# Attention and two expert layers in one kernel: the second pair's queries and keys ahead of the first weights, and the first chunk's tokens split block by block

## The chip, the cores and the metric

The kernel runs on one core of one Trainium2 chip. Times are device microseconds (us) of one execution, as the median of the runs shown; the trace of one further execution shows where its time goes. A core has five engines that run programs of their own and meet at semaphores: TensorE (PE, with PEld for the loading of its stationary operand), VectorE (DVE), ScalarE (ACT), GpSimd (POOL) and SyncE (SP). SP computes nothing here; it issues the transfers between the device's memory and the core's memory.

## The reference

```python
# q, k, v: (4, 8, 576, 64)  f32;  M_prev: (4, 8, 64, 64);  z_prev: (4, 8, 64);  beta: (8)
scores = q @ k.T / sqrt(64), causal;   a = softmax(scores);   local = a @ v
phi(x) = where(x > 0, x, exp(x) - 1) + 1
mem_out = (phi(q) @ M_prev) / (phi(q) @ z_prev + 1e-6)
g = sigmoid(beta);  attn = g * mem_out + (1 - g) * local          # per head
x = attn as (2304 tokens, 512)
x = (sigmoid(x @ w_gate) * (x @ w_val)) @ w_out                   # 512 -> 1536 -> 512
h = x @ w_in;  out = (h * clip(h + 3, 0, 6) / 6) @ moe2_w_out     # 512 -> 2048 -> 512
```

## The kernel before

Work on PE is written out by hand (a manual schedule for PE alone); the instructions of DVE, ACT, POOL and SP are put in order by the scheduler that builds the program, so an edit can move them far from where it stands in the code. Once built, each engine goes through its own list in order.

**Phase A** computes attention and, between its pieces, the first layer for the first chunks of tokens. Attention goes by *visits*: a visit is one pair of heads of one batch and one of two ranges of query rows (range 0: rows 0 to 319; range 1: rows 320 to 575). The first four visits are the four pairs of batch 0 in range 0, the next four the same pairs in range 1, then batch 1, and so on. A visit takes two *steps* of the loop in `phase_a`; `t` counts them, from 0. A step issues on PE the scores of one or two blocks of rows (`score_part`, L344, tiles `s`), the transposes of the weights of step t-3 (`transpose_bank`, L402, tiles `t`), the product with the values of step t-4 (`pv`, L426), and *fill*: units of the first layer (`moe`). A unit is three matmuls (`mm3`, L233 to L235), because a float32 operand is split into a high and a low part, and five units stand in a step while the first chunk is worked on (`FILL`). DVE takes the maximum of each row of scores out of PSUM (`row_max`, L324), ACT the exponentials (L362).

`load_visit(v)` issues the loads of a visit: the transposed queries and keys (`qk`, L257 and L258), for a batch's first visit the memory's norms (`zz`), the queries in natural layout (the first part of `aux`, L272, read by `prep_phi`, L297) and the values (L274). `w_load` issues the loads of a group of two blocks of weights into one of two stage buffers (`wst`, L142, 512 KB each); `w_convert` rebuilds the floats out of 64-bit patterns and splits them (L152 to L164). Nine groups are converted in phase A.

The first layer goes by chunks of 312 tokens. Chunk 0 needs batch 0's range 0 of all four pairs, so the last `pv` that it needs is that of visit 3, at t = 11. Each `pv` is copied out (`xpr`, L435), written to device memory (`xd`, L438 to L440) and read back as a block of 128 features (`xc`, L464); ACT and DVE split the block into its two parts (`split`, L228 and L229, tiles `xs0` to `xs3`, one for each pair of heads). `moe_x(c)` does that for all four blocks once `ready(c)` holds, and the first unit of the chunk may stand `LEAD` = 2 steps later. With these rules chunk 0's first unit stands at t = 14 and, after 72 units, its last at t = 28; chunk 1's blocks are asked for at t = 28 and its first unit stands at t = 30.

Phase B finishes the first layer, phase C computes the second.

Of the kernel before, what the change touches and what calls it, by code (L numbers as in the profile page):

```python
# [17 lines left out]
B, H, S, D = 4, 8, 576, 64  # L18
NT, DM = B * S, H * D
FF1, FF2 = 12, 16  # L20
KT = DM // 128
# [31 lines left out]
LAG, LEAD = 1, 2  # L53
# [25 lines left out]
class Kernel:  # L79
# [9 lines left out]
    def setup(self):  # L89
        nc, tc, ctx = self.nc, self.tc, self.ctx  # L90
        cp = self.pool(ctx, "const", 1)
        self.wpool = self.pool(ctx, "wslots", NW_A)
        self.xd = tc.dram_tile([KT, 128, NT], F32, name="xd")
        self.x2p = tc.dram_tile([KT, 128, NT], F32, name="x2p")
        self.x2 = tc.dram_tile([KT, 128, NT], F32, name="x2")
        self.wd = tc.dram_tile([NPAIR, 3, 128, 2048], F32, name="wd")
        self.bt_sb = cp.tile([128, H // 2 * 5], F32, name="bt_sb")
        nc.sync.dma_start(self.bt_sb, self.bt)
        self.three = cp.tile([128, 1], F32, name="three")
        nc.vector.memset(self.three, 3.0)  # L100

    def attn_consts(self, pool):
        nc = self.nc
        self.ident = pool.tile([128, 128], F32, name="ident")
        make_identity(nc, self.ident)
        self.mask = pool.tile([128, 576], F32, name="mask")
        nc.gpsimd.memset(self.mask, 0.0)
        nc.gpsimd.affine_select(
            out=self.mask[:, 448:576],
            in_=self.mask[:, 448:576],  # L110
            compare_op=ALU.is_ge,
            fill=-BIG,
            base=0,
            pattern=[[-1, 128]],
            channel_multiplier=1,
        )
        self.mask0 = pool.tile([128, 64], F32, name="mask0")
        for g in range(2):
            rows = slice(64 * g, 64 * g + 64)
            nc.gpsimd.tensor_copy(self.mask0[rows], self.mask[rows, 448 + 64 * g : 512 + 64 * g])  # L120
        self.a1 = pool.tile([128, H // 2 * 5], F32, name="a1")
        self.a2 = pool.tile([128, H // 2 * 5], F32, name="a2")
        nc.scalar.activation(self.a1, self.bt_sb, AF.Exp)
        nc.scalar.activation(self.a2, self.bt_sb, AF.Exp, scale=-1.0)
        nc.vector.tensor_scalar_add(self.a1, self.a1, 1.0)
        nc.vector.tensor_scalar_add(self.a2, self.a2, 1.0)
# [119 lines left out]
    def load_visit(self, v):  # L246
        if v >= len(VISITS):
            return
        nc = self.nc
        p, ranges = VISITS[v]  # L250
        b, h = PAIRS[p]
        qk = self.pa2.tile([128, 2, S], F32, name="qk", tag="qk")
        a = self.pa2.tile([128, 15 * D], F32, name="aux", tag="aux", bufs=3)
        rg = ranges[0]
        (t0, n), nb, j1 = RTOK[rg], len(ROWS[rg]), RANGES[rg][-1] + 1
        src = self.aux[b, h // 2]
        nc.sync.dma_start(qk[:, 0, t0 : t0 + n], self.qk[b, h // 2, :, 0, t0 : t0 + n])  # L257
        nc.sync.dma_start(qk[:, 1, : t0 + n], self.qk[b, h // 2, :, 1, : t0 + n])  # L258
        if h == 0 and rg == 0:
            z = self.pa2.tile([128, H + H // 2, D], F32, name="zz", tag="zz", bufs=1)  # L260
            flat = lambda t: t.rearrange("p h d -> p (h d)")
            one = lambda t: t.rearrange("o h d -> o (h d)")
            nc.sync.dma_start(flat(z[:, 0:H]), one(self.zz[b : b + 1, 0:H]).broadcast_to([128, H * D]))
            for g in range(2):
                h0 = H + H // 2 * g
                nc.sync.dma_start(
                    flat(z[64 * g : 64 * g + 64, H:]),
                    one(self.zz[b : b + 1, h0 : h0 + H // 2]).broadcast_to([64, H // 2 * D]),
                )
            self.z = z  # L270
        q0 = 0 if rg == 0 else 5 * D
        nc.sync.dma_start(a[:, 0 : nb * D], src[:, q0 : q0 + nb * D])  # L272
        v0 = 5 * D
        nc.sync.dma_start(a[:, v0 : v0 + j1 * 2 * D], src[:, 9 * D : 9 * D + j1 * 2 * D])  # L274
        self.visits[v] = {
            "pair": PAIRS[p],
            "ranges": ranges,
            "z": self.z,
            "qk": qk,
            "qn": a[:, 0 : nb * D].rearrange("p (r d) -> p r d", d=D),  # L280
            "v": a[:, 5 * D :].rearrange("p (j c) -> p j c", j=5),
        }
# [173 lines left out]
        need = (b, 0 if t1 < RTOK[0][1] else 1)  # L456
        return need in self.done and self.step >= self.done[need] + LAG

    def moe_x(self, c):

        xs = []
        for k in range(KT):
            x = self.pm2.tile([128, CA], F32, name="xc", tag="xc")
            self.nc.sync.dma_start(x, self.xd[k, :, c * CA : c * CA + CA])  # L464
            t = self.pm1.tile([128, 2, CA], F32R, name=f"xs{k}", tag=f"xs{k}")
            self.split(t[:, 0], t[:, 1], x, self.nc.scalar, self.nc.vector)
            xs.append((t[:, 0], t[:, 1]))
        self.xnext = (c, xs, self.step)

    def moe_a(self, c):  # L470

# [36 lines left out]
    def phase_a(self):  # L508
        nc, tc = self.nc, self.tc
# [6 lines left out]
        self.plan_weights(keys, [self.wpool] * NW_A)  # L516
        steps = [(v, rg, u[-1]) for v, (p, ranges) in enumerate(VISITS) for rg in ranges for u in UNITS[rg]]
        nt = len(steps)
        self.xnext = None
        stream, c = None, 0  # L520
        tq, vq = [], []

        def moe(k):
            nonlocal stream, c
            while k > 0:
                if stream is None:
                    if c == NCA:
                        return
                    if self.xnext is None or self.xnext[0] != c:
                        if not self.ready(c):  # L530
                            return
                        self.moe_x(c)
                    if self.step < self.xnext[2] + LEAD:
                        return
                    stream = self.moe_a(c)
                    c += 1
                try:
                    next(stream)
                    k -= 1
                except StopIteration:  # L540
                    stream = None

        def transposes(t, k):
            for _ in range(k):
                if tq and tq[0][0] <= t:
                    a = tq.pop(0)[1]
                    self.transpose_bank(*a)
                    if a[2] == len(BANKS[a[1]]) - 1:
                        vq.append((t + 1, a[:2]))

        t = self.step = 0
        sched = tc.manual_schedule(engines={mybir.EngineType.PE})
        sched.__enter__()
        self.load_visit(0)
        self.w_load()
        self.load_visit(1)
        while t < nt or tq or vq:
            self.step = t
            fill = FILL[max(c - 1, 0)]
            first = w = 0  # L560
            if t < nt:
                v, rg, i = steps[t]
                if i == UNITS[rg][0][-1]:
                    self.new_weights(v, rg)
                w = 64 + 128 * i
                first = w if w <= 512 else 320
                self.score_part(v, i, 0, first)
            if t == 0:
                self.prep_phi(0)
            if t < nt and i == RANGES[rg][-1]:  # L570
                self.memory_rows(v, rg)
            transposes(t, 2)
            if vq and vq[0][0] <= t:
                self.pv(*vq.pop(0)[1])
            if first < w or (tq and tq[0][0] <= t):
                moe(fill // 2)
                fill -= fill // 2
                if first < w:
                    self.score_part(v, i, first, w)
                transposes(t, 1)  # L580
            if t < nt:
                self.exponentials(v, i)
                if i == RANGES[rg][-1]:
                    self.normalize(v, rg, 5 <= t < 27)
                    tq += [(t + 3, (v, rg, j)) for j in range(len(BANKS[rg]))]
            moe(fill)
            if t < nt and i == UNITS[rg][0][-1]:
                self.load_visit(v + 2)
            if t < nt and i == RANGES[rg][-1]:
                self.prep_phi(v + 1)  # L590
            if t >= 5 and t % 2:
                self.w_convert()
            if len(self.wstaged) < 2:
                self.w_load()
            t += 1
# [20 lines left out]
        while c < NCA or stream is not None:  # L616
            self.step += 1
            moe(8)
            if n < NW_B - NLATE - 2:
                self.w_next()  # L620
                n += 1
# [352 lines left out]
```

## Time and profile before

| what | value |
|---|---|
| median of 3 runs (lowest to highest) | 1067.75 us (1067.61 to 1069.07) |
| the profiled execution's own time | 1067.68 us |
| its span in the trace | 1065.9 us |
| PE busy | 1029.6 us (97%) |
| DVE, ACT, POOL busy | 645.5 (61%), 550.8 (52%), 83.5 us (8%) |

The span is 1.8 us shorter than the time of the same execution, so a microsecond of the span is a microsecond of the time. Busy shares are means over the whole span; the first 60 us look different from the rest, and PE's few idle microseconds lie mostly there.

### The profile page before, as it was taken

How to read it: one execution, taken by the hardware profiler on the slowest of the kernel's cores; microseconds unless marked ns; L12 is line 12 of the kernel's file. 1: busy time of each engine (PE TensorE's matmuls, PEld its weight loads, DVE VectorE, ACT ScalarE, POOL GpSimd, SP SyncE). 2: the span in 40 equal slices, each digit the busy share in tenths (PEclk: the TensorE clock that was granted, in tenths of full speed). 3: DMA queues.
4: the chain of work that ended last, by engine and by line, in shares of the span. 5: the costliest groups of instructions: out<-in, count | busy, mean ns of one | idle time of the engine just before them, and what ended most of it. 6: DMA issues, size and time to landing. Idle time of an engine off the chain costs nothing.

```text
span 1065.9 us, 16031 instructions
## 1 busy us (share of the span) xinstructions
PE 1029.6 (97%) x5824; PEld 886.0 (83%) x5824; DVE 645.5 (61%) x1543; ACT 550.8 (52%) x1191; POOL 83.5 (8%) x102
## 2 busy tenths in 40 slices
PE   5689999999999999999999999999999999999998
PEld 3367678878887899999888888888888888888886
DVE  6989755454455438888888888743454433643432
ACT  5999875576556644435444343433453333633432
POOL 3212211110111000000000000310002000000000
PEclk9999999999999999999999999999999999999999
DMA  7756542424242215336686877444404542044511
GB/s 227 215 177 198 189 126 75 137 80 123 68 125 79 62 47 179 119 119 250 231 295 246 310 261 275 152 158 188 148 30 158 217 155 103 10 164 172 218 40 60
DMA packets 66239, 164.87 MB, mean 155 GB/s; under 512 B 8432, under 2 KB 41712, under 8 KB 60272
## 3 DMA queue, kind: packets, MB, share of 16 engines
q1 hardware_dynamic: 66160, 163.85, 44.8%
q8 instruction: 46, 0.75, 0.3%
q14 instruction: 33, 0.27, 0.1%
HBM read 122.76 MB, written 41.06 MB: 154 GB/s over the span
## 4 chain that ended last, share of the span: by engine, by line
PE 84%; DVE 5%; ACT 5%; DMA 4%; issue 1%; SPq 1%; POOL 1%; ACTq 0%; POOLq 0%; DVEq 0%
PE acc L822 18%; PE pa L787 9%; PE pb L787 7%; PE m L233 6%; PE m L234 5%; PE m L235 5%; PE g L235 5%; PE g L233 5%; PE g L234 5%; PE pv L426 4%; PE t L402 4%; PE s L344 3%; PE acc L234 2%; PE acc L235 2%; PE acc L233 2%; DMA aux<-in_aux 1%
## 5 line engine op out<-in xcount | busy, mean ns | idle before, releaser
L822 PE MATMUL acc<-wslot,hs 128*128 128x512 f32 x864 | 227.8, 395 | 2.2 <-ACT hs L228 2.2
L822 PEld LDWEIGHTS acc<-wslot,hs 128*128 128x128 f32 x864 | 159.5, 188 | 27.7 <-ACT hs L228 3.5
L787 PE MATMUL pa<-xq,wslot 128*128 128x384 f32 x576 | 117.3, 338 | 1.1 <-ACT u L887 0.6
L787 PEld LDWEIGHTS pa<-xq,wslot 128*128 128x128 f32 x576 | 103.7, 187 | 9.9 <-ACT u L887 0.9
L235 PE MATMUL g<-xs,wslot 128*128 128x468 f32 (+1 forms) x288 | 106.4, 370 | 0.0
L234 PE MATMUL g<-xs,wslot 128*128 128x468 f32 (+1 forms) x288 | 106.2, 369 | 0.0
L233 PE MATMUL g<-xs,wslot 128*128 128x468 f32 (+1 forms) x288 | 104.1, 369 | 0.0
L362 ACT ACTIVATE P<-P,m 128x192 f32<-128x192 f32 (+4 forms) x144 | 83.9, 584 | 31.1 <-DVE m L324 29.8
L233 PE MATMUL m<-xs,wslot 128*128 128x312 f32 x288 | 93.8, 326 | 0.3 <-DVE m L324 0.3
L234 PE MATMUL m<-xs,wslot 128*128 128x312 f32 x288 | 88.1, 306 | 0.0
L235 PE MATMUL m<-xs,wslot 128*128 128x312 f32 x288 | 87.9, 305 | 0.0
L787 PE MATMUL pb<-xq,wslot 128*128 128x384 f32 x432 | 87.8, 338 | 0.0
L787 PEld LDWEIGHTS pb<-xq,wslot 128*128 128x128 f32 x432 | 77.9, 188 | 6.3
L344 PE MATMUL s<-qk 64*128 64x320 f32 (+3 forms) x320 | 67.9, 494 | 13.6 <-DMA qk<-in_qk 10.8
L851 DVE TENSOR_TENSOR c<-pb,u 128x384 f32<-128x384 f32 x48 | 26.6, 555 | 87.0 <-ACT u L887 86.0
L799 ACT ACTIVATE r<-c,three 128x384 f32<-128x384 f32 x72 | 44.2, 613 | 63.0 <-DVE c L851 63.0
L402 PEld LDWEIGHTS t<-ident,P 128*128 128x128 f32 x464 | 52.8, 143 | 25.1 <-issue 14.9
L402 PE MATMUL t<-ident,P 128*128 128x128 f32 x464 | 67.2, 281 | 5.6 <-ACT T L404 2.7
L229 DVE TENSOR_TENSOR hs<-r,hs 128x384 fp32r<-128x384 f32 x96 | 55.8, 585 | 26.8 <-ACT hs L228 25.4
L324 DVE CUSTOM_DVE_ANT_0 P<-s,mask 128x320 f32<-128x320 f32 (+3 forms) x144 | 62.5, 452 | 12.9 <-PE s L344 12.5
L404 ACT COPY T<-t 128x512 f32<-128x512 f32 (+2 forms) x128 | 65.6, 540 | 8.8 <-PE t L402 8.7
L426 PE MATMUL pv<-T,aux 128*64 128x256 f32 (+2 forms) x512 | 61.3, 367 | 8.3 <-ACT T L404 8.3
(101 smaller groups left out, 1918.4 us busy)
## 6 DMA issues: line engine op xcount, KB each, us to landing
wst<-in_wm SPq DMA_DIRECT2D x68, 512.0 KB, 5.7
wslot<-wd SPq DMA_DIRECT2D x30, 1024.0 KB, 5.1
wd<-wslot SPq DMA_DIRECT2D x16, 1024.0 KB, 4.8
wslot<-wd SPq DMA_DIRECT2D x15, 768.0 KB, 6.2
wd<-wslot SPq DMA_DIRECT2D x8, 768.0 KB, 5.6
qk<-in_qk SPq DMA_DIRECT2D x32, 160.0 KB, 2.4
aux<-in_aux SPq DMA_DIRECT2D x16, 320.0 KB, 3.3
qk<-in_qk SPq DMA_DIRECT2D x16, 288.0 KB, 3.0
```

The source lines that it names most:

```text
L229: elo.tensor_tensor(lo, src, hi.bitcast(F32), op=ALU.subtract)
L233: nc.tensor.matmul(out, w[0], x[0], start=first, stop=False)
L234: nc.tensor.matmul(out, w[0], x[1], start=False, stop=False)
L235: nc.tensor.matmul(out, w[1], x[0], start=False, stop=last)
L324: self.nc.vector.tensor_tensor_reduce(out=self.row(v, rg, r, 64 + a, 64 + e), in0=ps, in1=mask, scale=-0.125, scalar=3.0e38 if a == 0 else ...
L344: nc.tensor.matmul(ps[:, : e - a], qk[rows, 0, q0 : q0 + 128], qk[rows, 1, a:e], start=True, stop=True)
L362: self.nc.scalar.activation(x, x, AF.Exp, bias=vs["m", rg][:, r : r + 1], scale=-1.0, accum_out=vs["l", rg][:, r : r + 1])
L402: nc.tensor.transpose(ps[:, 128 * n : 128 * n + 128], self.row(v, rg, r, 128 * j, 128 * j + 128), self.ident)
L404: nc.scalar.copy(pr["T", rg][:, 512 * k : 512 * k + c], ps[:, :c])
L426: nc.tensor.matmul(ps[rows, o : o + w], pr["v"][:, j, rows], T[:, c : c + w], start=(n == 0), stop=(n == last), skip_group_check=True,)
L787: nc.tensor.matmul(ps[:, :HC], w[:, i, b, cc], x[:, l, k], start=first and k == 0 and n == 0, stop=last and k == 1 and n == 2, skip_group_ ...
L822: nc.tensor.matmul(a, h[:, i, cc], w[:, l, f], start=first and f == 0 and n == 0, stop=last and f == 1 and n == 2)
```

## The change

Two places change. **Loads at the start:** the second visit's loads (`load_visit(1)`) are issued ahead of the first group of weights (`w_load`); in a visit the natural queries come ahead of the norms `zz`; the small `bt` and the two exponentials made of it (now in `gates`) come after the first visit's loads. **Chunk 0:** `moe_x` takes a list of blocks, and each block of chunk 0 is asked for one step after the `pv` of its pair; when the fourth is there, the first unit may stand 1 step later instead of 2.

```diff
     def setup(self):
-        nc.sync.dma_start(self.bt_sb, self.bt)
...
+    def gates(self):
+        nc, pool = self.nc, self.pa1
+        nc.sync.dma_start(self.bt_sb, self.bt)
         self.a1 = pool.tile([128, H // 2 * 5], F32, name="a1")
...
     def load_visit(self, v):
         nc.sync.dma_start(qk[:, 1, : t0 + n], self.qk[b, h // 2, :, 1, : t0 + n])
+        q0 = 0 if rg == 0 else 5 * D
+        nc.sync.dma_start(a[:, 0 : nb * D], src[:, q0 : q0 + nb * D])
         if h == 0 and rg == 0:
...
-        q0 = 0 if rg == 0 else 5 * D
-        nc.sync.dma_start(a[:, 0 : nb * D], src[:, q0 : q0 + nb * D])
...
-    def moe_x(self, c):
+    def moe_x(self, c, parts=range(KT)):
-        xs = []
-        for k in range(KT):
+        xs = self.xpart
+        for k in parts:
...
-        self.xnext = (c, xs, self.step)
+        if len(xs) == KT:
+            self.xnext, self.xpart = (c, xs, self.step), []
...
-                        if not self.ready(c):
+                        if c == 0 or not self.ready(c):
                             return
                         self.moe_x(c)
-                    if self.step < self.xnext[2] + LEAD:
+                    if self.step < self.xnext[2] + (LEAD if c else 1):
                         return
...
         self.load_visit(0)
+        self.gates()
+        self.load_visit(1)
         self.w_load()
-        self.load_visit(1)
...
             transposes(t, 2)
+            if first_x and first_x[0][0] <= t:
+                self.moe_x(0, [first_x.pop(0)[1]])
             if vq and vq[0][0] <= t:
-                self.pv(*vq.pop(0)[1])
+                u = vq.pop(0)[1]
+                self.pv(*u)
+                if u[0] < KT:
+                    first_x.append((t + 1, u[0]))
```

What the built programs' orders show, at three places. First SP, from its first transfer on (`bt_sb`, `qk`, `zz`, `aux`, `wst` as above), before:

```order
L98 DMA bt_sb<-in_bt 128x20
L257 DMA qk<-in_qk 128x320
L258 DMA qk<-in_qk 128x320
L263 DMA zz<-in_zz 128x512
L266 DMA zz<-in_zz 64x256 x2
L272 DMA aux<-in_aux 128x320
L274 DMA aux<-in_aux 128x384
L142 DMA wst<-in_wm 128x1024 x2
L257 DMA qk<-in_qk 128x320
L258 DMA qk<-in_qk 128x320
L272 DMA aux<-in_aux 128x320
L274 DMA aux<-in_aux 128x384
```

and SP of the changed kernel, from its first transfer on:

```order
L260 DMA qk<-in_qk 128x320
L261 DMA qk<-in_qk 128x320
L263 DMA aux<-in_aux 128x320
L268 DMA zz<-in_zz 128x512
L271 DMA zz<-in_zz 64x256 x2
L277 DMA aux<-in_aux 128x384
L123 DMA bt_sb<-in_bt 128x20
L260 DMA qk<-in_qk 128x320
L261 DMA qk<-in_qk 128x320
L263 DMA aux<-in_aux 128x320
L277 DMA aux<-in_aux 128x384
L145 DMA wst<-in_wm 128x1024 x2
```

The second visit's four transfers have moved ahead of the two of the weights, and `bt` behind the first visit's.

Second PE, from the scores of t = 13 on (`xs_632` is block 0 of chunk 0, `wslot` a group of converted weights), before:

```order
L344 MATMUL s<-qk 128x320 x2
L402 MATMUL t<-ident,P 128x128 x6
L344 MATMUL s<-qk 128x256 x2
L344 MATMUL s<-qk 128x448 x2
L402 MATMUL t<-ident,P 128x128 x8
L426 MATMUL pv<-T,aux 64x256 x8
L426 MATMUL pv<-T,aux 64x128 x2
L233 MATMUL m<-xs_632,wslot 128x312
L234 MATMUL m<-xs_632,wslot 128x312
L235 MATMUL m<-xs_632,wslot 128x312
```

and after (`xs_363`, `xs_455` and `xs_551` are blocks 0, 1 and 2):

```order
L347 MATMUL s<-qk 128x320 x2
L405 MATMUL t<-ident,P 128x128 x6
L236 MATMUL m<-xs_363,wslot 128x312
L237 MATMUL m<-xs_363,wslot 128x312
L238 MATMUL m<-xs_363,wslot 128x312
L236 MATMUL m<-xs_455,wslot 128x312
L237 MATMUL m<-xs_455,wslot 128x312
L238 MATMUL m<-xs_455,wslot 128x312
L347 MATMUL s<-qk 128x256 x2
L236 MATMUL m<-xs_551,wslot 128x312
```

Five units (15 matmuls) have moved into t = 13, ahead of the scores of t = 14 (128x448); the steps 14 to 26 hold five units as before, and five units are missing at t = 27 and t = 28. Chunk 1 still starts at t = 30.

Third DVE, around the split of chunk 0's last block `xs3_647`, before (the slots of the first five groups of weights are `wslot_323`, `413`, `504`, `595` and `709`):

```order
L324 ISA P_722,m_724<-s_725,mask_100 128x448
L324 ISA m_724 128x1
L308 SCALAR_TENSOR_TENSOR nr_587<-nr_587,a2_109 128x4
L309 RECIPROCAL nr_587<-nr_587 128x4
L324 ISA P_722,m_724<-s_727,mask_100 128x448
L324 ISA m_724 128x1
L158 ISA wst_423<-wst_423,wf_596 128x1024x2
L229 TENSOR_TENSOR xs3_647<-xc_645,xs3_647 128x312
L164 TENSOR_TENSOR wslot_595<-wst_423,wslot_595 128x1024
```

and after (the first five slots are `wslot_323`, `418`, `514`, `610` and `728`):

```order
L327 ISA P_623,m_625<-s_694,mask_99,m_625 128x256
L327 ISA m_625 128x1
L161 ISA wst_524<-wst_524,wf_729 128x1024x2
L232 TENSOR_TENSOR xs3_647<-xc_645,xs3_647 128x312
L167 TENSOR_TENSOR wslot_728<-wst_524,wslot_728 128x1024
L388 SCALAR_TENSOR_TENSOR l_624<-l_624,a1_120 128x4
L389 RECIPROCAL l_624<-l_624 128x4
L327 ISA P_741,m_743<-s_744,mask_99 128x448
L327 ISA m_743 128x1
```

Before, the split of the last block stood behind both row maxima of t = 14 and in front of the last instruction for the fourth group of weights. Now it stands ahead of the row maxima of t = 14, and in front of the last instruction for the fifth group.

On SP, further on, the read of block 3 (`xc`) came directly behind the last of that block's writes (`xd`), with the fifth group of weights (`wst`) one place ahead of that write. Now the two loads of the sixth group stand between the last write and the read. With two stage buffers the sixth group's load waits for the last instruction for the fourth group on DVE, which stands 24 places ahead of the split of `xs3`.

## Rows read from the trace of the kernel before

**Rows 1.** The page: the span, and each engine's busy time.

```profile
span 1065.9 us, 16031 instructions
PE 1029.6 (97%) x5824; PEld 886.0 (83%) x5824; DVE 645.5 (61%) x1543; ACT 550.8 (52%) x1191; POOL 83.5 (8%) x102
```

**Rows 2.** Stretches: length, each engine's busy us, granted clock, DMA share, GB/s.

```profile
5.00:10.00 5.00, 2.25 (x12) 0.79 (x8) 2.49 (x12) 2.93 (x11) 0.85 (x2) 1.00 0.89 242
10.00:15.00 5.00, 1.39 (x8) 0.95 (x8) 3.82 (x15) 1.35 (x4) 0.88 (x2) 1.00 0.93 325
5.00:20.00 15.00, 8.64 (x45) 5.68 (x43) 11.22 (x42) 8.22 (x25) 3.66 (x5) 1.00 0.87 283
20.00:60.00 40.00, 28.78 (x180) 16.04 (x180) 38.85 (x122) 38.93 (x94) 10.67 (x13) 0.96 0.68 207
75.00:127.00 52.00, 51.52 (x375) 40.26 (x370) 46.86 (x129) 46.91 (x124) 13.09 (x15) 1.00 0.64 206
127.00:147.00 20.00, 17.57 (x103) 11.54 (x104) 10.57 (x45) 15.48 (x38) 2.69 (x4) 0.91 0.42 123
147.00:1066.00 919.00, 910.38 (x5050) 802.69 (x5046) 525.75 (x1177) 425.12 (x881) 50.55 (x54) 1.00 0.42 148
```

**Rows 3.** Timeline, 4 to 14 us: start, length, instruction, [idle before <- releaser].

```profile
4.93 0.91 SPq L142 DMA_DIRECT2D wst<-in_wm  x2
...
5.59 0.36 DVE L324 CUSTOM_DVE_ANT_0 P<-s,mask 128x192 f32<-128x192 f32 x1 [2.61 <-PE s L344]
...
12.68 1.12 ACT L152 ACTIVATE wf<-wst 128x1024 f32<-128x1024 f32 x1 [2.57 <-DMA wst<-in_wm]
...
13.61 1.14 PE L344 MATMUL s<-qk 64*128 64x192 f32 x4 [6.36 <-DMA qk<-in_qk]
```

**Rows 4.** Timeline, 52 to 64 us: the last block's way, and its first use.

```profile
52.00 0.45 SPq L440 DMA_DIRECT2D xd<-xpr  x1
...
56.55 0.33 SPq L464 DMA_DIRECT2D xc<-xd  x1
...
60.16 0.46 ACT L228 CAST xs<-xc 128x312 fp32r<-128x312 f32 x1
...
61.15 0.47 DVE L229 TENSOR_TENSOR xs<-xc,xs 128x312 fp32r<-128x312 f32 x1
...
62.16 0.30 PE L233 MATMUL m<-xs,wslot 128*128 128x312 f32 x1
...
63.11 0.81 PE L344 MATMUL s<-qk 64*128 64x320 f32 x4
```

**Rows 5.** DVE: nine conversions (tile wf, then wslot: DVE third), and a row maximum.

```profile
12.00:120.00 108.00, 41.28 (x45) 10.45 (x9) 0.98 0.63 197
...
12.00:120.00 108.00, 28.59 (x166) 24.02 (x167) 11.55 (x9) 10.34 (x9) 0.98 0.63 197
...
L324 DVE CUSTOM_DVE_ANT_0 P<-s,mask 128x448 f32<-128x448 f32 x16 | 9.7, 616 | 0.3 <-PE s L344 0.3
```

**Rows 6.** Timeline of PE, at t = 15, 16, 26, 27 and 30.

```profile
68.20 1.11 PE L344 MATMUL s<-qk 64*128 64x256 f32 x4 [2.61 <-DVE m L324]
...
70.72 0.59 PE L344 MATMUL s<-qk 64*128 64x192 f32 x2
...
123.04 1.02 PE L344 MATMUL s<-qk 64*128 64x448 f32 x4
...
127.49 0.81 PE L344 MATMUL s<-qk 64*128 64x320 f32 x4
...
131.23 1.90 PE L426 MATMUL pv<-T,aux 128*64 128x320 f32 x10 [2.24 <-ACT T L404]
...
144.32 1.07 PE L402 MATMUL t<-ident,P 128*128 128x128 f32 x8 [0.19 <-ACT T L404]
...
147.41 0.41 PE L233 MATMUL m<-xs,wslot 128*128 128x312 f32 x1
```

**Rows 7.** The page, DMA issues: KB each, median us from issue to landing.

```profile
wst<-in_wm SPq DMA_DIRECT2D x68, 512.0 KB, 5.7
```

More of the change, by code (lines that the diff above doesn't have):

```diff
@@ L518, in phase_a @@
         nt = len(steps)
-        self.xnext = None
+        self.xnext, self.xpart = None, []
         stream, c = None, 0
-        tq, vq = [], []
+        tq, vq, first_x = [], [], []
         def moe(k):
```

## The prediction, on record before the changed kernel was run

> **What bounds the kernel now.** I read the page first: PE is busy for 1029.6 of the span's 1065.9 us [rows 1], so it idles 36 us, and only there can a change of order gain anything. The windows tell where. From 147 us to the end PE is busy for 910.4 of 919 us, and in 75 to 127 for 51.52 of 52; the stretches up to 60 us leave it idle for 6.4 of 15 and 11.2 of 40 us [rows 2]. But there another engine takes over: in 20 to 60 DVE is busy for 38.85 of 40 us and ACT for 38.93. So the reader is to see three stages: to 60 us DVE and ACT set the pace (attention and the conversion of weights at once), from 75 us on PE does, and in 127 to 147 nobody does quite: PE 17.57 of 20, at a granted clock of 0.91.
>
> Then the timeline of the start: PE's scores at t = 2 wait 6.36 us for the second visit's `qk` and begin at 13.61, while the first weights were issued at 4.93 and reach ACT at 12.68 [rows 3]. This is the wait that the first edit is about. DVE has its first row maximum at 5.59, and between there and 60 it idles 15 − 11.22 + 40 − 38.85, less the 0.59 up to 5.59, that is 4.34 us. These 4.34 us, and not PE's 6.36, are all that an earlier start can give as long as DVE bounds.
>
> Last, where the change ends. Behind t = 29 every engine has the same list in both kernels, so what counts is how far the first unit of t = 30 moves; it begins at 147.41 [rows 6]. I follow the shift from the start to there.
>
> **The change part by part.** *Loads at the start.* The weights' 1.05 MB no longer go ahead of the second `qk`. At the 325 or 242 GB/s of 10 to 15 and 5 to 10 us [rows 2] these are 3.2 or 4.3 us, so PE's scores of t = 2 begin at 9.3 to 10.4; I take 9.8, 3.8 us earlier. The weights come later by 1.2 us (`qk` alone, 0.33 MB at the 283 GB/s of 5 to 20) to 2.4 us (with `aux`, 0.69 MB). DVE has row maxima to do in the meantime, so of its 4.34 us of idleness some stay: at least 0.5 (it can't have work at once behind its first maxima), at most all. I take 1.5, since the third visit's loads are now behind the weights and will be waited for. Saved: 4.34 − 1.5 = 2.8 us, bounds 0 and 3.8. `bt` and the exponentials behind the first visit's loads cost nothing: their first reader on DVE comes many row maxima later. The two exponentials would cost only their few hundredths if that cover were gone.
>
> *Conversions.* The scheduler moved them forward. Ahead of the split of `xs3` DVE had three conversions and five of the six instructions of a fourth; now it has four and five of a fifth. One more costs 41.28/9 + 11.55/9 = 4.59 + 1.28 = 5.87 us [rows 5]. The two row maxima of t = 14 now stand behind the split, 2 × 0.62 = 1.23 us. Together +4.64, against −2.84: the split moves from 61.15 [rows 4] to 62.95 and ends at 63.4 instead of 61.6. So the fourth block is there later, not earlier, although its unit now stands one step earlier.
>
> *PE around t = 13 to 16.* At t = 13 PE now has units 1 to 3, and unit 4 needs `xs3`. Behind it waits everything that PE does for t = 14 and 15. Before, the same unit (the fourth of t = 14 then) began at 62.16, unhindered, and the scores of t = 16 began at 70.72, 8.56 us later, with 2.61 us of waiting for a row maximum: 5.95 us of work [rows 4, 6]. Now come besides, between the arrival of `xs3` and t = 16: five units, of which six matmuls took 63.11 − 62.16 = 0.95 us, so 15 take 2.4; t = 14's scores, 1.02 as at 123.04; its transposes and values, 3.1 as from 144.32 to 147.41; and some four more transposes, 0.2 (an estimate: eight took 1.07, with part of them counted already). Sum 6.7. In return the 2.61 us of waiting go, since DVE's row maxima are done while PE works. PE's t = 16 comes at 63.4 + 5.95 + 6.7 = 76.0 instead of 70.7: +5.3 us.
>
> *t = 16 to 27.* Both kernels have five units in a step here and PE bounds: in 75 to 127 it idles 0.48 us [rows 2]. DVE (46.86 of 52) and ACT (46.91) have a conversion less before them now, so that the 0.48 may go too: −0.5.
>
> *t = 27 to 30.* Before, this took 147.41 − 127.49 = 19.92 us. The five units that moved forward, 2.4 us, are missing there now; a wait of 2.24 us for ACT's copy of `T` at 131.23 [rows 6] may end, as everything but PE has had time to run ahead; and the granted clock of 0.91 cost up to 9% of 20, 1.8 us. At most 2.4 + 2.24 + 1.8 = 6.4 us come back, at least none: chunk 1 may not start before t = 30, so where DVE and ACT set the time of t = 28 and 29, missing units leave a hole and no gain. PE's 17.57 of 20 says that both engines' chains are near; I take the half, −3.2.
>
> **Sum.** The profiled execution's own time, 1067.68 (0.07 below the median, 1.8 above its span), + 5.3 − 0.5 − 3.2 = **1069.3 us**, 0.15% above the median. What a measurement of this kernel can tell from no change is about 0.2%, 2.1 us: this is no change.
>
> **The rivals.** *The block comes late by its transfer (slower).* Between block 3's last write and its read stand the sixth group's two loads, and these wait for the fourth group's conversion. Back from the split at 62.95, DVE has five instructions of a conversion (4.65 us), two row maxima of 448 (1.23) and four smaller ones with the small operations of t = 12 (some 2.8, an estimate from the same rows): so the loads go at about 54.2, the read at 55.0 behind SP's 0.8 us. Before, the read was issued at 56.55 and ACT had its block by 60.16, 3.6 us later at most [rows 4]. If the two loads pass ahead of it in the 3.2 us worked out above, DVE can split at 55.0 + 3.2 + 3.6 + 0.5 = 62.3, just in time; if they take the 5.7 us that a load of 512 KB takes from issue to landing [rows 7], it is 64.8, 1.8 us late, and the time is 1071.1; if both take that in turn, 70.5 and 1076.8. It decides from a landing at about 62.4 on. For it: the margin is 0.6 us. Against it: sixteen engines share the loads, and the read need not be last on each.
>
> The Trainium skill, "DMA: Bandwidth & Descriptors", section "Anatomy of one DMA — SWDGE (gpsimd) path", puts a transfer at about 2.0 us fixed plus its bytes at 436 GB/s; it is measured on GpSimd's path, and this queue is SP's. By it the loads would take some 2.4 us and the read as much (an estimate from that page), and this rival would be nothing. The trace doesn't agree: the last write, 64x64 floats issued at 52.00, let its read go only at 56.55, after 4.55 us [rows 4].
>
> *Both soft terms at their good ends (faster).* DVE's idleness falls to 0.5, so 3.8 us are saved at the start and the split stands at 62.0: −1.0. And all 6.4 us of t = 27 to 30 come back: −3.2. Then 1069.3 − 4.2 = 1065.1. For it: PE's idle time before 147 is 27 us, and a PE that has done its units a step earlier has less left to do while DVE and ACT are ahead. Against it: those engines are busy 97% of the time where the delay arises, and the pause at t = 28 and 29 has a fixed step as its end.
>
> *The first edit doesn't do what it says.* `qk` is still late, because transfers share the queue and SP goes on only as earlier ones land; nothing of DVE's 4.34 us is saved: +2.8, 1072.1. For it: PE waits 6.36 us for a transfer issued within a microsecond or two of the weights. Against it: in 5 to 15 us the DMA engines are busy for 0.89 and 0.93 [rows 2], so it is bytes that are waited for, and these have moved.
>
> **How the numbers follow.** I give my forecast 0.41 (its own range 1067 to 1071), the late block 0.22, the good ends 0.31, the ineffective edit 0.06. Faster by over 0.2% (below 1065.6) is most of the good ends (0.24) and a little of the forecast (0.04): 0.28. Slower (above 1069.9) is 0.16 of the late block, 0.05 of the ineffective edit and 0.10 of the forecast: 0.31. The rest, 0.41, is the same. The range goes from 1064.4, 0.7 us beyond the good ends for the estimated transposes and the start's spread of ±0.5, to 1073.0: there the return of t = 27 to 30 is nothing (+3.2) with some lateness of the block, or the block is late by 1.8 and the start saves half. That leaves about 0.1 on each side.
>
> **What would show it.** Right: scores of t = 2 at 9.3 to 10.4 with a wait for `qk` of 2 to 3 us; DVE idle about 1.5 us before 60; PE waiting at t = 13 ahead of unit 4 for `xs3`, split by DVE at about 63 directly behind the fifth group's fifth instruction; t = 16 at about 76, t = 27 at about 132, t = 30's first unit near 149. Wrong: DVE waiting ahead of that split for ACT or the transfer (late block); the wait for `T` gone and t = 27 to 30 in 14 us or less (good ends); scores of t = 2 at 13 (ineffective). The prediction falls altogether if PE is kept from t = 14 by something other than `xs3`, such as a conversion that isn't done when its units come, or if DVE's order meets waits that I cannot see from before.

## The result, and the profile after

The changed kernel takes 1076.1 us (1074.8 to 1076.75, four runs) where the kernel before took 1067.99 beside it: a ratio of 1.0065 [1.0049, 1.0081]. The forecast was 1069.3, so it is 6.8 us beyond it and above the range. The profiled execution spans 1074.5 us, 8.6 more than before.

First PE's timeline at the start and from t = 13 on, in the changed kernel (start, length, instruction; in brackets the idle time before it and what ended it).

```profile
9.70 1.14 PE L347 MATMUL s<-qk 64*128 64x192 f32 x4 [3.26 <-DMA qk<-in_qk]
...
15.70 1.10 PE L347 MATMUL s<-qk 64*128 64x192 f32 x4 [3.09 <-DMA qk<-in_qk]
...
57.22 0.81 PE L347 MATMUL s<-qk 64*128 64x320 f32 x4
60.23 0.66 PE L405 MATMUL t<-ident,P 128*128 128x128 f32 x4 [2.20 <-ACT T L407]
...
66.04 0.63 PE L236 MATMUL m<-xs,wslot 128*128 128x312 f32 x1 [0.53 <-ACT xs L231]
67.34 0.63 PE L237 MATMUL m<-xs,wslot 128*128 128x312 f32 x1 [0.68 <-DVE xs L232]
...
68.94 1.87 PE L347 MATMUL s<-qk 64*128 64x448 f32 x4
...
82.14 0.59 PE L347 MATMUL s<-qk 64*128 64x192 f32 x2
...
139.77 0.81 PE L347 MATMUL s<-qk 64*128 64x320 f32 x4
...
155.28 0.41 PE L236 MATMUL m<-xs,wslot 128*128 128x312 f32 x1
```

The rows at 9.70, 66.04, 82.14, 139.77 and 155.28 answer to those at 13.61, 62.16, 70.72, 127.49 and 147.41 of before [rows 3, 4, 6]. PE starts 3.9 us earlier and is then 11.4 us late at t = 16, 12.3 at t = 27 and 7.9 at t = 30. So the time is lost before t = 16, and a third of it is given back behind t = 27. The row at 57.22, the first scores of t = 13, answers to this one of before:

```profile
49.44 0.81 PE L344 MATMUL s<-qk 64*128 64x320 f32 x4
```

PE was 7.8 us late there already, before it came to any unit of chunk 0. For the last block it waited only 0.53 and 0.68 us, at 66.04 and 67.34, the second time for DVE's half of the split:

```profile
66.81 0.48 DVE L232 TENSOR_TENSOR xs<-xc,xs 128x312 fp32r<-128x312 f32 x1
```

Then the windows of the changed kernel: each engine's busy time (PE, PEld, DVE, ACT, POOL), granted clock, DMA share, GB/s.

```profile
5.00:10.00 5.00, 1.74 (x8) 0.84 (x8) 2.83 (x16) 3.35 (x13) 1.72 (x3) 1.00 0.84 229
10.00:15.00 5.00, 2.61 (x12) 1.12 (x11) 4.58 (x19) 2.12 (x8) 1.02 (x2) 1.00 0.97 301
4.59:66.81 62.22, 41.64 (x202) 23.38 (x200) 55.93 (x167) 50.03 (x123) 16.06 (x18) 0.88 0.68 217
62.00:66.00 4.00, 3.51 (x15) 2.15 (x13) 3.47 (x13) 4.00 (x8) 0.61 (x1) 0.58 0.37 128
66.00:74.00 8.00, 7.29 (x30) 4.62 (x32) 5.80 (x12) 8.00 (x17) 0.00 (x0) 0.57 0.50 159
```

and the same kind of row for the kernel before, from DVE's first row maximum to its split of `xs3`:

```profile
5.59:61.15 55.56, 37.98 (x228) 22.52 (x227) 51.22 (x163) 48.30 (x121) 14.48 (x18) 0.97 0.72 224
```

The third row and this one are the pair to read. Ahead of the split DVE works 55.93 us instead of 51.22 and idles 6.29 instead of 4.34. The rows at 62 to 74 show the second thing: PE's granted clock is near half, mostly its lower level (1.2 GHz), while PE at last has work; before, 60 to 75 us was at full clock (1.00). The scores of t = 14 take 1.87 us there, against 1.02 for the same shape at full clock [rows 6]. The kernel before had such a stretch too, only sooner: its own scores of t = 14, at 54.66, took 1.7 us at a granted clock of 0.52 (53.6 to 57 us).

### The profile page after: what moved, and what is told of

It is laid out like the page before. It is cut to its first block, busy times and chain, and to the rows that moved or that the text cites. A ratio compares the mean times of both kernels' runs of the same rounds, so it can differ in the third digit from the quotient of the medians.

```text
span 1074.5 us, 16035 instructions
## 1 busy us (share of the span) xinstructions
PE 1037.0 (97%) x5824; PEld 889.4 (83%) x5824; DVE 647.1 (60%) x1543; ACT 551.4 (51%) x1191; POOL 84.0 (8%) x102
## 4 chain that ended last, share of the span: by engine, by line
PE 86%; DVE 5%; ACT 3%; DMA 3%; issue 1%; SPq 1%; POOL 1%; ACTq 0%; DVEq 0%; POOLq 0%
PE acc L832 18%; PE pa L797 9%; PE pb L797 7%; PE m L236 6%; PE g L238 5%; PE g L236 5%; PE g L237 5%; PE m L237 5%; PE m L238 5%; PE pv L429 4%; PE t L405 4%; PE s L347 4%; PE acc L237 3%; PE acc L238 3%; PE acc L236 3%
## 5 line engine op out<-in xcount | busy, mean ns | idle before, releaser
L347 PE MATMUL s<-qk 64*128 64x320 f32 (+3 forms) x320 | 71.3, 512 | 10.6 <-DMA qk<-in_qk 10.0
L429 PEld LDWEIGHTS pv<-T,aux 128*64 128x64 f32 x512 | 35.9, 140 | 41.4 <-ACT T L407 19.2
```

The source lines that it names most:

```text
L347: nc.tensor.matmul(ps[:, : e - a], qk[rows, 0, q0 : q0 + 128], qk[rows, 1, a:e], start=True, stop=True)
L429: nc.tensor.matmul(ps[rows, o : o + w], pr["v"][:, j, rows], T[:, c : c + w], start=(n == 0), stop=(n == last), skip_group_check=True,)
```

## The experiments

Ratios are to runs of the kernel before on the same chip. They are grouped by the question they answer.

### Which of the two edits, and where the first unit stands

Theory A was that a fifth conversion ahead of the split and DVE's idleness make the split late; theory B that PE's wait for the last block at t = 13, with t = 14 behind it, is the loss. The four corners: loads old or new, first unit at t = 13 or 14. `e1_loads` leaves out the edit to chunk 0, `e2_blocks` the edit to the loads; `e3_lead2` and `e4_blocks_lead2` put the first unit back to t = 14, with new and with old loads:

```diff
 # e1_loads: new loads, chunk 0 asked for at once
-                        if c == 0 or not self.ready(c):
+                        if not self.ready(c):
...
-                    if self.step < self.xnext[2] + (LEAD if c else 1):
+                    if self.step < self.xnext[2] + LEAD:
...
-            if first_x and first_x[0][0] <= t:
-                self.moe_x(0, [first_x.pop(0)[1]])
...
 # e2_blocks: old loads, blocks one by one
         self.load_visit(0)
-        self.gates()
+        self.w_load()
         self.load_visit(1)
-        self.w_load()
...
 # e3_lead2: as changed, and e4_blocks_lead2: as e2_blocks, both with
-                    if self.step < self.xnext[2] + (LEAD if c else 1):
+                    if self.step < self.xnext[2] + LEAD:
```

(In `e2_blocks` and `e4_blocks_lead2`, `bt` and the queries also stand where they stood before.)

> The new order of loads alone; chunk 0 is asked for at once and its first unit stands at t = 14, as before. Here four groups of weights are converted ahead of the split of the last block, as in the changed kernel (three before). Theory A (the conversion moved ahead, and the idleness that the new loads leave on DVE, make the split late; where the unit stands matters little): 1071 to 1075 us. Theory B (what costs is that PE waits for the split at t = 13 with the scores of t = 14 behind it, so that its clock falls): 1066 to 1069 us.

> The block-by-block chunk 0 alone, its first unit at t = 13, with the loads of before. Only three groups are converted ahead of the split of the last block, and that split stands ahead of both row maxima of t = 14. Theory A: not slower, 1064 to 1068 us. Theory B: 1071 to 1076 us, with the granted clock at half speed around the first units.

> The changed kernel, but the first unit one step later (t = 14), so that the scores of t = 14 stand ahead of PE's wait for the last block. Theory A: within 2 us of the changed kernel, 1074 to 1077 us. Theory B: 1067 to 1070 us, clock at full speed from 60 us on.

> Loads of before, blocks asked for one by one, first unit at t = 14. The rest of the order is that of before. Both theories: as before, 1067 to 1069 us; it is the corner that the other three are compared with, and it shows what asking for blocks early does by itself (it can save little, since the last block is asked for in the same step).

Measured: `e1_loads` 1.0011 [1.0, 1.0022], `e2_blocks` 1.0041 [1.0026, 1.0056], `e3_lead2` 1.0048 [1.0031, 1.0065], `e4_blocks_lead2` 1.0002 [0.9992, 1.0013]. So neither theory holds alone. Asking for blocks early costs nothing by itself; the new loads gain nothing by themselves; the unit at t = 13 costs 0.4% even with old loads (`e2_blocks` against `e4_blocks_lead2`), where only three groups are converted ahead of the split and it is early, at 60.35. PE's timeline of `e2_blocks`:

```profile
59.66 0.63 PE L234 MATMUL m<-xs,wslot 128*128 128x312 f32 x1 [4.50 <-ACT xs L229]
61.30 0.63 PE L235 MATMUL m<-xs,wslot 128*128 128x312 f32 x1 [1.01 <-DVE xs L230]
62.89 1.86 PE L345 MATMUL s<-qk 64*128 64x448 f32 x4
```

There PE waits 5.5 us in two pieces for the last block and the scores of t = 14 take 1.86 us behind it. That is theory B. But `e3_lead2`, which has no such wait, loses as much: there attention itself is late (scores of 256 columns of t = 13 at 61.18, before 53.64) and the clock is 0.51 in 60 to 70 us. Its trace is to be read with care: it is of the slowest of its six runs (1078.52 us, median 1073.97), and 4 of its 11 us of lateness at t = 30 arise behind t = 16, where a unit at 89.8 us starts after a wait of 3.35 us that DVE ended.

### Is it the conversion that moved ahead?

`e5_gate`, `e6_gate_lead2` and `e7_gate_loads` are the changed kernel, `e3_lead2` and `e1_loads` with a dependence that holds the fifth group's conversion behind the split of the last block.

```diff
+        self.nconv = getattr(self, 'nconv', -1) + 1
+        if self.nconv == 4:
+            nc.vector.tensor_copy(w[:, 0, 0:1], self.xnext[1][3][1][:, 0:1].bitcast(F32))
         nc.scalar.activation(w, hif, AF.Abs)
```

> The changed kernel, but the conversion of the fifth group has to wait for the split of the last block (one tiny copy from it, ahead of the conversion). Ahead of that split DVE then has 5 of 6 instructions of a conversion less (4.6 us) and the two row maxima of 256 columns at t = 13 less (some 0.9 us), so the split should come at about 61 us instead of 66.8. If the moved conversion is the main loss (theory A): 1069 to 1072 us. If what counts is that PE waits at t = 13 at all (theory B): 1073 to 1077 us, since PE still waits there.

> The same gate, with the first unit at t = 14, where PE has the scores of t = 14 to do ahead of it. Theory A: 1067 to 1070 us, since the earlier start is kept and the split is no later than before; theory B: the same, and at least 3 us below the gate with the unit at t = 13. If both are wrong (the loss is DVE's idleness under the new loads): 1072 to 1075 us.

> The new loads alone (chunk 0 asked for at once, first unit at t = 14), with the gate on the fifth group. Without the gate that was 1070.3 us. If the conversion that moved ahead costs there too: 1066 to 1069 us, at or below the kernel before; if it doesn't: 1070 to 1072 us.

Measured: 1.0056 [1.0037, 1.0076], 1.005 [1.0031, 1.007] and 1.0075 [1.0051, 1.0099]. Theory A falls as far as the conversion goes: DVE works 51.66 us ahead of the split instead of 55.93, yet the split comes at 65.31 instead of 66.81, where about 61 was expected. DVE's timeline of `e5_gate` shows why:

```profile
65.31 0.48 DVE L235 TENSOR_TENSOR xs<-xc,xs 128x312 fp32r<-128x312 f32 x1 [2.97 <-ACT xs L234]
```

DVE has the time now and waits 2.97 us for ACT's half of the same split, which stands in ACT's list behind the exponentials and the normalization of attention. DVE and ACT reach this place by a chain of attention steps, and the chain is late, not DVE's own work alone. In `e7_gate_loads` PE also waited 1.89 and 3.41 us at 122 to 126 us for a late group of weights, so its time is not the gate's alone.

### Does the half clock cost by itself?

`e8_warm` adds matmuls that nobody reads, where PE waits at t = 13:

```diff
                 self.score_part(v, i, 0, first)
+                if t in (13,):
+                    w0 = self.w[1, 0, 0]
+                    ps = self.ps_m.tile([128, 512], F32, name="m", tag="m")
+                    for n in range(14):
+                        nc.tensor.matmul(ps[:, :CA], w0[:, 0, :128], w0[:, 0, :CA], start=True, stop=True)
```

> The changed kernel with 14 idle matmuls of 128x312 (their result is read by nobody) behind the first scores of t = 13, where PE waits 2.2 us. They add about 2 us of PE's work at full clock. If the fall of the granted clock behind that wait is a part of the loss: the clock stays at full speed from 62 to 74 us and the time falls by 2 to 4 us, to 1072 to 1074. If the clock costs nothing there, because DVE and ACT are late anyhow: 1075 to 1078 us.

Measured: 1073.61 us, 1.0041 [1.0027, 1.0056]. That is 2.5 us below the changed kernel, as expected of the clock, but it decides nothing: the interval overlaps the changed kernel's, the granted clock only moved its low stretch (0.86 in 60 to 70, 0.80 in 70 to 80), t = 16 comes no earlier (82.58), and the scheduler changed DVE's order with it. What the clock costs is read from rows instead, below.

### The same orders, held

The scheduler rebuilds the lists of DVE, ACT and POOL with every edit. To part the edits from that, order edges (no waits) hold these lists:

```diff
+    def pin(self):
+        edge = mybir.DependencyInfo(mybir.DependencyClass.NoSync, mybir.DependencyReason.DATA)
+        for name, text in ORDER.items():
+            mine = [i for i in self.nc.cur_bb.bb.instructions if i.engine == getattr(mybir.EngineType, name) and type(i).__name__.startswith("Inst")]
+            row = [mine[int(k)] for k in text.split()]
+            for a, b in zip(row, row[1:]):
+                self.tc.add_manual_dep(b, a.name, edge, reason="order")
...
+        self.pin()
         att_ctx.close()
```

`ORDER` lists the instructions by number. `e9_loads_order` is `e1_loads` in the order of before, `e10_old_loads_new_order` is `e2_blocks` in the order of the changed kernel, `e11_after_old_order` the changed kernel in the order of before.

> The new loads alone, first unit at t = 14, and DVE, ACT and POOL held in the order of the kernel before (order edges without waits; only the additions and exponentials of bt stand some places later, as their load does). Theory C (what costs is the order that the scheduler rebuilt around the new loads: weights converted and copies made at other places between the steps of attention): 1063 to 1068 us, below the kernel before, since the earlier start is kept. Theory D (the loads themselves cost, weights and the third visit's loads coming later): 1070 to 1074 us, as or above the new loads with their own order (1070.3).

> The loads of before with the block-by-block chunk 0 (first unit at t = 13), and DVE, ACT and POOL held in the order of the changed kernel. With their own order these loads gave 1074.0 us. Theory C: as the changed kernel or above, 1075 to 1080 us. Theory D: at most 1074 us.

> The changed kernel, with DVE, ACT and POOL held in the order of the kernel before up to the split of the last block, which alone moves ahead of the two row maxima of t = 14 (it has to, since PE has it ahead of the scores of t = 14); behind it the scheduler is free. Only three groups of weights are converted ahead of it. Theory C: 1066 to 1070 us, some 6 to 10 us below the changed kernel. Theory B (PE's wait at t = 13 and its clock): 1071 to 1076 us, with a wait of 2 us or more ahead of unit 4 and the clock at half speed behind it.

Measured: 0.9998 [0.9985, 1.0011], 1.0086 [1.0065, 1.0106] and 1.0072 [1.0052, 1.0091]. Three readings. The order of before, held up to the split, doesn't save the changed kernel as long as five units stand at t = 13 (`e11_after_old_order`, 1078.05), so theory C, the scheduler's order as the main loss, falls. The order isn't free either: `e10_old_loads_new_order` came out as theory C expected, and its 1.0086 lies clear of the 1.0041 that the same loads and units gave in their own order. And the new loads gain nothing in the order of before; theory D's loss doesn't appear, but here are ACT and DVE of `e9_loads_order`:

```profile
14.55 1.12 ACT L207 ACTIVATE wf<-wst 128x1024 f32<-128x1024 f32 x1 [4.52 <-DMA wst<-in_wm]
...
15.70 0.69 DVE L208 TENSOR_SCALAR wf<-wf 128x1024 f32<-128x1024 f32 x1 [2.95 <-ACT wf L207]
```

PE has its scores of t = 2 at 9.08 there, 4.5 us earlier than before. DVE waits 2.95 us for the weights, and PE has the scores of t = 4 at 16.96, 0.65 us later than before (16.31).

### Three units at t = 13 instead of five

This leaves units 1 to 3, whose blocks are there, at t = 13 and puts unit 4 behind the attention of t = 14, so PE no longer waits ahead of it.

```diff
-            fill = FILL[max(c - 1, 0)]
+            fill = 3 if t == 13 else FILL[max(c - 1, 0)]
```

`e14_three_units` is that edit in the changed kernel. `e12_three_units_order` adds the order of before up to the split of the last block, `e13_three_units_old_loads` has old loads as well; `e15_three_units_weights` (old loads) and `e16_three_units_new_loads` hold the order through the eighth conversion.

> New loads and block-by-block chunk 0, but only three units (the first three blocks) at t = 13: unit 4, which needs the last block, stands at t = 14 behind the scores, transposes and values of t = 14. DVE, ACT and POOL in the order of the kernel before up to the split of the last block. Against the same order with five units at t = 13 (1078.05 us) only PE's order differs. If PE's wait for the last block ahead of t = 14 is the loss (theory B): 1067 to 1071 us. If the loss is something else about asking for blocks early or about units at t = 13: 1075 to 1079 us.

> The same three units at t = 13 and the same order, with the loads of before: nothing is moved but nine matmuls, into an idle stretch of PE. Theory B: 1066 to 1069 us, at most 1.4 us below the kernel before (nine matmuls of 0.158 us leave the stretch that PE bounds). If moving units to t = 13 costs in itself: 1071 us or more.

> The changed kernel with three units at t = 13 instead of five, all orders left to the scheduler. Theory B with the rest of the loss in the scheduler's order: 1071 to 1074 us, between the new loads alone (1070.3) and the changed kernel (1076). If the wait costs nothing beside that order: 1075 to 1077 us.

> Three units at t = 13 with the loads of before, as in the last run, but the order of before is held for DVE, ACT and POOL as far as the eighth conversion, not only up to the split of the last block. There PE was 1.8 us ahead of the kernel before at t = 16 and 2.7 us at t = 23, and lost it at 115 us, waiting 4.07 and 2.69 us for the eighth group of weights, which the scheduler had put later between the steps of attention. Theory B: the waits for weights go and what PE was ahead by stays: 1064 to 1067 us, below the kernel before. If the weights are late in any order, because DVE and ACT can't convert them sooner: 1069 to 1073 us.

> The same as the last run (three units at t = 13, order of before through the eighth conversion), with the new loads. Against the run with five units at t = 13 in that order (1078.05 us) the wait for the last block ahead of t = 14 is gone, and the wait for the eighth group of weights is held as small as the order of before makes it. If the wait at t = 13 is the larger part of the changed kernel's loss: 1069 to 1073 us. If it is not: 1075 to 1079 us.

Measured: `e12_three_units_order` 1.0078 [1.0057, 1.0099], `e13_three_units_old_loads` 1.006 [1.0043, 1.0078], `e14_three_units` 1.0054 [1.0033, 1.0076], `e15_three_units_weights` 1.0027 [1.0016, 1.0039], `e16_three_units_new_loads` 1.0042 [1.0026, 1.0057]. By their times, `e12_three_units_order` (1077.96 us) and `e13_three_units_old_loads` (1076.23) fall where theory B is wrong, and `e14_three_units` (1074.93, between its two ranges), the changed kernel without its wait for the last block, can't be told from the changed kernel (1.0065 [1.0049, 1.0081]). With old loads three units in the order of before are no better than five in their own order (`e2_blocks`, 1.0041). PE's timelines show what becomes of the wait. First t = 16 of `e11_after_old_order` (five units), then of `e12_three_units_order` (same loads, and the same order up to the split but for the two row maxima of t = 14), then of `e14_three_units`:

```profile
86.22 1.01 PE L365 MATMUL s<-qk 64*128 64x192 f32 x4
...
72.68 0.76 PE L365 MATMUL s<-qk 64*128 64x192 f32 x4
...
79.04 1.29 PE L347 MATMUL s<-qk 64*128 64x192 f32 x4
```

Next `e13_three_units_old_loads` at the eighth group of weights:

```profile
115.34 0.63 PE L252 MATMUL m<-ha,wslot 128*128 128x312 f32 x1 [4.07 <-ACT wslot L182]
...
118.91 0.63 PE L254 MATMUL m<-ha,wslot 128*128 128x312 f32 x1 [2.69 <-DVE wslot L183]
```

and `e15_three_units_weights` at the same weights:

```profile
116.72 0.41 PE L261 MATMUL m<-ha,wslot 128*128 128x312 f32 x1 [3.14 <-DVE wslot L190]
```

In the order of before, the loss at t = 16 goes with the wait at t = 13: 13.5 us between `e11_after_old_order` and `e12_three_units_order` (their lists differ behind the split, and the traces are of the slowest run of the one and the fastest of the other), and with old loads PE is 1.8 us ahead of before (68.92). In the changed kernel's own order it is different: without any wait for the last block t = 16 comes at 79.04, 3.1 us earlier than 82.14 and still 8.3 later than before, at a granted clock of 0.72 in 62 to 74 us, and at t = 30 only 0.3 us of the 3.1 are left (154.96 against 155.28). Its scores of t = 13 begin at 57.18, as late as in the changed kernel.

In `e13_three_units_old_loads` all of the gain is lost again at 115 to 119 us, where PE stands still for 6.8 us until the eighth group is converted. Holding that conversion's place shortens the wait to 3.1 us but doesn't remove it: DVE finishes the group at about 116.7 us there (115.45 + 1.22), as it did before (115.20 + 1.23), where PE came later and waited for none. So the last conversions are a second bound right behind the first. What the wait at t = 13 with its clock costs in whole times stays open: `e2_blocks` against `e4_blocks_lead2` gives 0.4%, `e11_after_old_order` against `e16_three_units_new_loads` 0.3% with orders held to different places, `e11_after_old_order` against `e12_three_units_order` and the changed kernel against `e14_three_units` nothing that can be told from noise. None of the sixteen is measurably below the kernel before.

## Why the prediction was wrong, step by step

**Where it ended.** The forecast's chain, term by term, against the profiled execution:

| step | forecast | measured | from |
|---|---|---|---|
| split of `xs3` against 61.15 | +1.8 (62.95) | +5.7 (66.81) | DVE's timeline |
| DVE's work ahead of it | +4.64 | +4.71 | windows, 55.93 − 51.22 |
| DVE's idleness ahead of it | 1.5 | 6.29 | windows, 62.22 − 55.93 |
| unit 4 to the scores of t = 16 | 12.65 | 14.80 | 82.14 − 67.34 |
| t = 16 against 70.72 | +5.3 | +11.4 | PE's timeline |
| t = 16 to 27, change | −0.5 | +0.9 | 57.63 − 56.77 |
| t = 27 to 30, change | −3.2 | −4.4 | 15.51 − 19.92 |
| from t = 30 on | 0 | +0.7 | 919.2 − 918.5 |
| sum | +1.6 | +8.6 | spans |

In this chain two terms were mis-sized, and they make 6.1 of the 7.0 us: the split came 3.9 us later than forecast (4.8 us more idleness, less 1.0 us of an earlier start that was not counted), and the way from unit 4 to t = 16 took 2.15 us more. The outline was right: a later split, t = 14 behind unit 4 and late with it, part of the loss given back at t = 27 to 30. But PE was not mainly held by the split. It came to t = 13 7.8 us late (57.22 against 49.44), waited 2.20 and 0.84 us for ACT's copies of `T` (2.50 before), and then 1.2 us in all for the last block. The prediction had named "PE is kept from t = 14 by something other than `xs3`" as a sign against itself, and so it was for the greater part: attention on PE, ACT and DVE was late as a whole, and without any wait for the last block 8.3 of the 11.4 us at t = 16 remain (`e14_three_units`). Nor is the sum of DVE's work and idleness a cause: with the fifth conversion's work taken out (`e5_gate`), DVE waited for ACT instead.

**The step that failed** is DVE's idleness under the new loads: "of its 4.34 us of idleness some stay", of which "I take 1.5". It was 6.29. `qk` came when forecast (9.70; forecast 9.8), yet DVE got 1.0 us from an earlier first item and nothing more. The start waits for bytes: from 5 to 15 us 2.65 MB are moved now, 2.84 before (229 + 301 and 242 + 325 GB/s over 5 us each), with the DMA engines busy for 0.84 and 0.97 of the time (0.89 and 0.93 before). Moving one load ahead put others back. The weights reach ACT at 14.78 instead of 12.68, the third visit's `qk` holds PE for 3.09 us at 15.70, where before nothing waited, so that of 3.9 us 0.6 are left there. In `e9_loads_order` this is seen alone, with no gain left. Up to 20 us DVE idled 3.15 us, as before (3.19): waits for the first visit's queries (`aux`, 1.21) and the first weights (0.99) are gone, and waits for the queries of the second and third visit (1.12 and 0.53) and smaller ones for PE and ACT have come. I had named the waits for later loads but priced them at 1.0 us, and taken 4.3 us only as the far bound. That idleness can rise above what it was, I had excluded without a reason. Behind 20 us DVE idled 3.14 us where it was 1.15 before: 1.64 for POOL's part of the norms (0.80 and 0.84), 1.00 for ACT (0.16, 0.49 and 0.35), little for PE (0.18). Attention's chain of PE, ACT, POOL and DVE is slower in the new order; PE's clock is lower there too, 0.78 from 34 to 57 us where it was 0.93. With old loads the same order is late as well (`e10_old_loads_new_order`, t = 16 at 84.03). Why it is slower no run shows.

**Then the clock.** The 12.65 us from unit 4 to t = 16 were worked out from rows at full clock. The granted clock was 0.58 and 0.57 in 62 to 74 us, with waits of 2.20 and 0.84 us ahead of that stretch and of 0.53 and 0.68 us in it. Instructions of the same shape took 1.87 instead of 1.02 us (scores of t = 14) and 1.97 instead of 1.09 (eight transposes). These two rows alone are 1.7 of the 2.15 us beyond forecast. This is read from rows; the experiment meant to show it (`e8_warm`) did not. The low clock isn't due to the wait for the last block alone: `e14_three_units` has none and 0.72 in 62 to 74 us.

**The rivals.** The late block by its transfer was wrong, although its worst case, 1076.8 us, came nearest to the time: that is luck. The read went at 59.59, behind the two loads, and landed 3.9 us later, where it had taken 2.2 before; that was 2 us ahead of ACT's cast at 65.54, which waited for nothing. The Trainium skill, "DMA: Bandwidth & Descriptors", "Anatomy of one DMA — SWDGE (gpsimd) path", gives about 2.4 us for this read (an estimate: 2.0 fixed and 160 KB at 436 GB/s). Its path is another one; the measured 3.9 decides, and it was in time by either. By the same fit of the Trainium skill the prediction's 2.4 us for a load of 512 KB should read 3.2 (an estimate); the two loads took 3.5 and 4.3. Its "few hundredths" for the two exponentials are 0.22 and 0.20 us in the trace of before. Neither changes its sum. The good ends were half right: 4.4 of at most 6.4 us came back at t = 27 to 30. The ineffective edit was right that nothing would be saved and had the wrong reason: `qk` was early.

**What stays open.** Why `e3_lead2` is 0.48% slower with no wait for the last block at t = 13, while `e1_loads`, which differs only in when the blocks are asked for, is 0.11%: in the one the clock is 0.51 in 60 to 70 us, in the other 1.00, but no run holds the order fixed between them. And how the changed kernel's loss divides between the late attention and the wait: each alone gives 0.4 to 0.5% (`e3_lead2`, `e2_blocks`), both together 0.65% with an interval that overlaps theirs, and taking the wait out of the changed kernel gave nothing clear of noise (`e14_three_units`, 0.54%).

## What to carry to other kernels

In this stretch, where the DMA engines were busy for 0.8 to 1.0 of the time, putting one load ahead of another only chose which wait was seen; count the bytes up to the first work of every engine before pricing the wait as a gain. Before a unit is moved a step earlier, look at what stands behind it in its engine's fixed list: an instruction whose operand is the last to arrive holds up everything behind it that is ready (5.5 us in `e2_blocks`). Three early units that had their operands brought PE to t = 16 sooner than five of which one waited, but no whole time shows a gain from it. So ask what is second in line: here the weights needed at 115 us took back all that the better start had won.

## What the runs showed of the hardware

- The granted clock can fall around waits of a few microseconds and stay low into the work behind them. In `e2_blocks` PE waited 4.50 us ahead of 59.66 and had 0.50 of the clock from 60 to 66 us, so that matmuls of 128x312 were listed with 0.63 us (the first of a group) and 0.47 where they have 0.41 and 0.30 at full clock [rows 4, 6]. There the wait cost more than its own length. Not every wait does this: in `e12_three_units_order` PE waited 1.80 us at 55.6 and 0.86 at 60.5, and the clock was 1.00 from 50 to 70 us.
- Up to the split of the last block `e11_after_old_order` and `e12_three_units_order` have the same loads and, but for the two row maxima of t = 14, the same list on DVE; six matmuls (0.95 us) stand at another place on PE. They reach t = 16 13.5 us apart. In the changed kernel's own order the same move is worth 3.1 us there (`e14_three_units`).
- Run to run, the kernel before spread from 1065.24 to 1073.46 us over all its executions; differences of 1 us were seen only by the ratio of many runs.
